# Two-layer decode kernel with backward pass: PSUM tiles of one bank for transposes, another order of zero stores and of streamed output-projection chunks, and vectors loaded as rows

## The chip, the core and the metric

The kernel runs on one NeuronCore of a Trainium2 chip. The metric is the device time of one execution in microseconds (us), as the median of several runs. One execution was also recorded by the hardware profiler; its trace gives the start and the length of every instruction and of the data transfers (DMA).

The engines named below are TensorE (PE, matrix multiplication; its weight loads are listed apart as PEld), VectorE (DVE), ScalarE (ACT), GpSimd (POOL) and SyncE (SP). Each has an instruction stream of its own and runs it in order. SP and ACT issue one kind of DMA queue, POOL another. PSUM, the memory that TensorE writes to, has 8 banks of 2 KiB per partition, and 128 partitions.

## The reference

One token (batch 1, sequence 1, width D = 1024) goes through attention, MLP, attention, MLP, each with a layer norm ahead and a residual sum behind, and both attentions use the same weights, as do both MLPs. The output and the gradients of everything but one unused input are returned.

```python
def _A_ref(x, k_cache, v_cache, wq, wo):          # Hq=32, Hkv=4, Sk=32768, Dh=128
    W = min(4096, max(256, Sk // 4))              # 4096: only the last W keys are used
    q = (x @ wq) ...                              # wq 1024 x 4096
    k = jnp.repeat(k_cache[:, :, Sk - W:, :], rep, axis=1); v = ...
    p = softmax(q k^T * Dh ** -0.5);  o = p v
    return o.reshape(B, Sq, Hq * Dh) @ wo         # wo 4096 x 1024
def _B_ref(x, w1, b1, w2):                        # F = 3584
    h = x @ w1 + b1;  act = h * tanh(softplus(h))
    return act @ w2
x = x + _A_ref(_layernorm(x), ...);  x = x + _B_ref(_layernorm(x), ...)
x = x + _A_ref(_layernorm(x), ...);  x = x + _B_ref(_layernorm(x), ...)
_out, _vjp = jax.vjp(_f, A_x, A_k_cache, A_v_cache, A_wq, A_wo, B_w1, B_b1, B_w2)
return (_out, *_vjp(grad_out))
```

All data are bf16. The gradients of the two caches have 4 x 32768 x 128 elements each, of which only the last 4096 positions of each head group are not zero; the other 28672 positions have to be written as zeros.

## The kernel before

The kernel has five parts, run one after the other by the data they need: the forward layers A1 (attention), B2 (MLP), A3 (attention), B4 (MLP); the backward layers B4, A3, B2, A1; and at the end the weight gradients, which are outer products of vectors kept from the layers (the "gradient part" below). Every vector of a layer is a column over 128 partitions.

**Weights.** wq, K and V are loaded once and stay in SBUF; so do the first 8 of 16 chunks of wo (`NR = 8`). The other 8 chunks of wo, and all of w1 (16 chunks of 448 KB) and w2 (14 chunks of 512 KB), are streamed anew in every layer through a pool `strm` of `NB = 5` buffers. SP issues these loads in the order of the program, each as soon as its buffer is free, so the first five chunks of a stage are requested before the stage begins.

**Forward.** `fwd_rows2` (L258) multiplies a chunk by a vector: 16 weight loads and 16 matmuls with one column each. In A1 and A3 the loop over the 16 wo chunks goes from 0 to 15, the kept ones first.

**Backward.** The backward products need the transposed chunks. `xpose2` (L153) transposes 16 blocks of 128x128 on TensorE into one PSUM tile of two banks, and then two copies (`evac`, L126), each of half the tile, bring them back into the same SBUF buffer; `evac` gives each copy to DVE or ACT by running sums of cost numbers. The backward stages (`mlp_bwd_w2`, `mlp_bwd_w1`, `attn_bwd`) run as a pipeline of lag 1: transposes of chunk i, then the products of chunk i-1. wq, K and V are transposed once for the backward pass: `attn_fwd` of A3 puts 32 such groups into a list `xq`, and `fill(n)` (L182) takes n from it. In the kernel before, 8 are taken between the wo chunks of A3 and 24 between the w1 chunks of B4 forward.

**PSUM.** Pool `p2` has 3 tiles of two banks, used for transposes, for the attention scores (`big`) and for small things; `pacc` holds two accumulators of one bank. For the gradient part `pacc` is released and a fourth two-bank tile takes its place.

**Zeros.** The 2 x 28672 x 4 zero rows are 112 stores of 512 KB from one SBUF tile `zt`. `zeros(n)` (L120) issues the next n of them on SP, so they stand in SP's queue among the loads. Where they stand is written out in the program: a table `Z` for the place after the fifth load of a stage, and single stores in the loops. The stores that are left go out at `zeros(1000)` behind the last backward layer.

**Gradient part.** Its pieces come in the order w2 (14 output tiles of 512 KB), b1, w1 (16 of 448 KB), wo (16), V cache (8), K cache (8), wq (16). Each tile is made by TensorE in PSUM, copied by DVE and ACT to one of 10 SBUF tiles, and stored by a DMA that POOL issues. `rows_put` (L585) prepares the vectors of a piece.

**Vectors.** x, grad_out and b1 are loaded straight into columns, by DMAs whose pieces are one or two elements long; the gradient of b1 is stored in the same way.

## Time and profile before

| | |
|---|---|
| median of 3 runs | 590.47 us (587.74 to 594.37) |
| profiled execution | 590.49 us; its span, first to last instruction, 588.5 us |
| busy: PE, DVE, ACT, POOL | 391.1, 227.7, 193.7, 51.6 us |
| DMA | 188.74 MB, mean 321 GB/s |
| mean granted TensorE clock | 0.67 of full speed |

Busy shares are averages over stages that are very unlike: long stages in which data streams in, chains of small dependent instructions, and the gradient part, which mostly writes. The DMA row of the profile's 40 slices (14.7 us each) and the rows of single stages say more. "[2.40 <-DMA w_c<-in_B_w_dram]" behind a row means that the engine was idle for 2.40 us ahead of it and that this load ended the wait; "issue" stands for idle time in which it waited for nothing that the profile shows.

The landmarks in the trace before, from DVE's rows: output of A1 at 74.83 us, of B2 at 115.60, of A3 at 164.29, of B4 at 232.09; end of the four backward layers at about 263, 317, 377 and 431 us; then the gradient part until 588.5.

### The profile page before, as it was taken

How to read it: one execution, taken by the hardware profiler on the slowest of the kernel's cores; microseconds unless marked ns; L12 is line 12 of the kernel's file. 1: busy time of each engine (PE TensorE's matmuls, PEld its weight loads, DVE VectorE, ACT ScalarE, POOL GpSimd, SP SyncE). 2: the span in 40 equal slices, each digit the busy share in tenths (PEclk: the TensorE clock that was granted, in tenths of full speed). 3: DMA queues.
4: the chain of work that ended last, by engine and by line, in shares of the span. 5: the costliest groups of instructions: out<-in, count | busy, mean ns of one | idle time of the engine just before them, and what ended most of it. 6: DMA issues, size and time to landing. Idle time of an engine off the chain costs nothing. (4 is left out here: it accounts for less than half of the span.)

```text
span 588.5 us, 15785 instructions
## 1 busy us (share of the span) xinstructions
PE 391.1 (66%) x7052; PEld 309.9 (53%) x7052; DVE 227.7 (39%) x409; ACT 193.7 (33%) x211; POOL 51.6 (9%) x95
## 2 busy tenths in 40 slices
PE   2375634476889789779679877886665313878871
PEld 2264533355879789668659866783611001136510
DVE  1033001012346633445422434333066415776692
ACT  1022000001436433435202333230055614755591
POOL 2000000000000000000000000000022212233341
PEclk9997555555869887979756889675555555555555
DMA  8999999993499698994921889999999999998886
GB/s 278 298 421 411 332 374 361 406 412 146 143 359 405 243 355 304 339 353 160 338 91 46 290 256 321 377 335 418 415 417 419 420 171 421 420 407 306 282 322 255
DMA packets 54883, 188.74 MB, mean 321 GB/s; under 512 B 9760, under 2 KB 9760, under 8 KB 53792
## 3 DMA queue, kind: packets, MB, share of 16 engines
q1 hardware_dynamic: 41648, 147.87, 67.4%
q0 software_dynamic: 10320, 39.86, 18.2%
q8 instruction: 55, 0.90, 0.6%
q10 hardware_dynamic: 2848, 0.01, 0.3%
q14 instruction: 12, 0.10, 0.1%
HBM read 89.14 MB, written 98.58 MB: 319 GB/s over the span
## 5 line engine op out<-in xcount | busy, mean ns | idle before, releaser
L177 PEld LDWEIGHTS <-w_c 128*128 128x128 bf16 x1792 | 59.2, 100 | 42.7 <-DMA w_c<-in_B_w_dram 23.8
L158 PE MATMUL tps<-ident_bf,w_c 128*128 128x128 bf16 x896 | 71.5, 244 | 12.7 <-DMA w_c<-in_B_w_dram 12.7
L132 ACT COPY w_c<-tps 128x1024 bf16<-128x1024 bf16 (+1 forms) x50 | 46.2, 927 | 82.7 <-DVE w_c L129 39.6
L129 DVE COPY w_c<-tps 128x1024 bf16<-128x1024 bf16 (+1 forms) x70 | 45.4, 667 | 67.7 <-PE tps L158 36.8
L158 PEld LDWEIGHTS <-w_c 128*128 128x128 bf16 x896 | 61.8, 111 | 14.0 <-DMA w_c<-in_B_w_dram 13.9
L132 ACT CAST st_t<-ops 128x1024 bf16<-128x1024 f32 x32 | 31.6, 1014 | 25.4 <-PE ops L177 19.7
L129 DVE CAST st_t<-ops 128x1024 bf16<-128x1024 f32 x28 | 33.6, 1223 | 9.7 <-issue 3.3
L177 PE MATMUL ops<-R_7920 2*128 2x512 bf16 (+1 forms) x64 | 11.1, 544 | 28.8 <-DVE st_w_8051 L129 6.4
L177 PE MATMUL acc<-a_pair,w_c 128*128 128x1 bf16 x448 | 15.7, 165 | 15.7 <-DMA w_c<-in_B_w_dram 10.3
L177 PE MATMUL acc<-nB_pair,w_c 128*128 128x1 bf16 x448 | 16.2, 165 | 14.4 <-DMA w_c<-in_B_w_dram 11.4
L158 PE MATMUL tps<-ident_bf,wo_c 128*128 128x128 bf16 x256 | 22.1, 256 | 3.6 <-DMA wo_c<-in_A_wo_dram 3.6
L177 PEld LDWEIGHTS <-wo_c 128*128 128x128 bf16 x512 | 16.7, 101 | 11.2 <-DMA wo_c<-in_A_wo_dram 6.9
L129 DVE COPY wo_c<-tps 128x1024 bf16<-128x1024 bf16 x20 | 13.5, 689 | 23.4 <-PE tps L158 16.0
L579 POOL DMA_DIRECT2D out_dram<-rt x2 | 1.2, 594 | 241.8 <-DVE rt L578 241.8
L129 DVE CAST st_kv<-ops 128x1024 bf16<-128x1024 f32 x15 | 18.3, 1224 | 9.9 <-PE ops L177 7.0
L177 PEld LDWEIGHTS <-R_7920 2*128 2x128 bf16 x64 | 2.3, 100 | 37.3 <-issue 37.3
L132 ACT CAST st_kv<-ops 128x1024 bf16<-128x1024 f32 x17 | 17.0, 1014 | 14.1 <-PE ops L177 14.1
L177 PE MATMUL acc<-dh_pair,w_c 128*128 128x1 bf16 x448 | 18.3, 165 | 4.8 <-ACT w_c L132 3.3
L158 PEld LDWEIGHTS <-wo_c 128*128 128x128 bf16 x256 | 19.1, 117 | 4.0 <-DMA wo_c<-in_A_wo_dram 4.0
L132 ACT COPY wo_c<-tps 128x1024 bf16<-128x1024 bf16 x12 | 12.1, 1012 | 25.6 <-DVE wo_c L129 17.1
L177 PE MATMUL ops<-Ro 2*128 2x512 bf16 x64 | 17.0, 603 | 5.0 <-ACT st_t L132 3.0
L634 POOL DMA_DIRECT2D out_dram<-st_t x30 | 16.0, 534 | 32.3 <-DVE st_t L129 14.1
(492 smaller groups left out, 711.4 us busy)
## 6 DMA issues: line engine op xcount, KB each, us to landing
out_dram<-zt SPq DMA_DIRECT2D x112, 512.0 KB, 10.0
w_c<-in_B_w_dram SPq DMA_DIRECT2D x64, 448.0 KB, 5.7
w_c<-in_B_w_dram SPq DMA_DIRECT2D x42, 512.0 KB, 6.1
wo_c<-in_A_wo_dram SPq DMA_DIRECT2D x32, 512.0 KB, 6.7
out_dram<-st_t POOLq DMA_DIRECT2D x30, 512.0 KB, 11.9
out_dram<-st_kv POOLq DMA_DIRECT2D x16, 512.0 KB, 5.7
out_dram<-st_wq POOLq DMA_DIRECT2D x16, 512.0 KB, 4.8
K_170<-in_A_k_cache_dram SPq DMA_DIRECT2D x1, 1024.0 KB, 13.3
```

The costliest lines, as they stand in the source:

```text
L129: nc.vector.tensor_copy(out_ap, in_ap)
L132: nc.scalar.copy(out_ap, in_ap)
L158: nc.tensor.transpose(ps[:, 8 * i + b, :], ap, ident_bf[:])
L177: nc.tensor.matmul(out_ap, lhsT=lhsT, rhs=rhs, start=start, stop=stop, skip_group_check=True, **kw)
L579: nc.gpsimd.dma_start(out_flat.rearrange("(n p) -> n p", p=P), rt[0:n, :])
L634: nc.gpsimd.dma_start(out_v[c], st[:])
```

## The change

1. **PSUM.** `p2` is gone until the gradient part. In its place stand `pt` with four tiles of one bank, and `pbig` with one tile of two banks for the scores. `xpose2` now takes one one-bank tile for each half (8 blocks), so that a half can be copied when its own 8 transposes are done. Ahead of the gradient part `pacc`, `pbig` and `pt` are released and `p2` is made with four tiles of two banks.
2. **Zeros.** The same 112 stores stand at other places: 6 in A1 (0 before), 18 in A3 (14), 15 among the w1 chunks of B4 forward (9), 2 in each backward w1 stage (4), 19 in the backward w2 stage of B2 (1), 4 in the attention backward of A1 (8); B2 (1), w2 of B4 (6) and the attention backward of A3 (8) keep theirs. What is left for the end is 31 stores (57 before).
3. **wo order.** The loop over wo in A1 and A3 takes chunks 8 to 15 (streamed) first and 0 to 7 (kept) then. No `fill` stands in that loop; B4 forward takes two groups for each of its 16 w1 chunks.
4. **Vectors.** x, grad_out and b1 are loaded as rows of 256 or 512 bytes at the start, transposed on TensorE and copied out of PSUM. The gradient of b1 is made ahead of the gradient part, transposed, and stored as 14 rows of 512 bytes.

SP's queue around the wo chunks of A1, from the last kept chunk on. `wo_c`, `w_c` are streamed chunks, `out_dram<-zt` is a zero store. Before:

```order
33 L244 DMA wo_200<-in_A_wo_dram 128x2048
34 L244 DMA wo_c<-in_A_wo_dram 128x2048 x8
35 L255 DMA w_c<-in_B_w_dram 128x1792 x5
36 L122 DMA out_dram<-zt 128x2048
37 L255 DMA w_c<-in_B_w_dram 128x1792 x11
```

And now:

```order
33 L255 DMA wo_210<-in_A_wo_dram 128x2048
34 L255 DMA wo_c<-in_A_wo_dram 128x2048 x5
35 L129 DMA out_dram<-zt 128x2048 x6
36 L255 DMA wo_c<-in_A_wo_dram 128x2048 x3
37 L266 DMA w_c<-in_B_w_dram 128x1792 x5
38 L129 DMA out_dram<-zt 128x2048
```

Six stores now stand between the fifth and the sixth streamed chunk. The same queue from A3's streamed wo chunks to the first w1 chunks of B4 forward. Before:

```order
39 L244 DMA wo_c<-in_A_wo_dram 128x2048 x5
40 L122 DMA out_dram<-zt 128x2048 x14
41 L244 DMA wo_c<-in_A_wo_dram 128x2048 x3
42 L255 DMA w_c<-in_B_w_dram 128x1792 x2
43 L122 DMA out_dram<-zt 128x2048
44 L255 DMA w_c<-in_B_w_dram 128x1792 x2
```

And now:

```order
41 L255 DMA wo_c<-in_A_wo_dram 128x2048 x5
42 L129 DMA out_dram<-zt 128x2048 x18
43 L255 DMA wo_c<-in_A_wo_dram 128x2048 x3
44 L266 DMA w_c<-in_B_w_dram 128x1792 x3
45 L129 DMA out_dram<-zt 128x2048
46 L266 DMA w_c<-in_B_w_dram 128x1792
47 L129 DMA out_dram<-zt 128x2048
```

Four more stores stand ahead of the sixth wo chunk, and from the third w1 chunk on each load has a store behind it. The queue at the end of A3's backward attention (`wo_c`) and in the backward w2 stage of B2 (`w_c`, 128x2048). Before:

```order
94 L244 DMA wo_c<-in_A_wo_dram 128x2048
95 L122 DMA out_dram<-zt 128x2048
96 L249 DMA w_c<-in_B_w_dram 128x2048 x5
97 L122 DMA out_dram<-zt 128x2048
98 L249 DMA w_c<-in_B_w_dram 128x2048 x9
```

And now:

```order
102 L255 DMA wo_c<-in_A_wo_dram 128x2048
103 L129 DMA out_dram<-zt 128x2048
104 L260 DMA w_c<-in_B_w_dram 128x2048 x5
105 L129 DMA out_dram<-zt 128x2048 x19
106 L260 DMA w_c<-in_B_w_dram 128x2048 x9
```

Nineteen stores instead of one stand between the fifth and the sixth w2 chunk. The core of the diff:

```diff
@@ -69,7 +69,8 @@
-    p2 = ctx.enter_context(tc.tile_pool(name="p2", bufs=3, space=bass.MemoryType.PSUM))
+    pt = tc.alloc_tile_pool(name="pt", bufs=4, space=bass.MemoryType.PSUM)
+    pbig = tc.alloc_tile_pool(name="pbig", bufs=1, space=bass.MemoryType.PSUM)
@@ -91,18 +92,24 @@
-    x0b = keep.tile([P, TD], BF16, name="x0b")
-    nc.sync.dma_start(x0b[:], A_x[0, 0, :].rearrange("(t p) -> p t", p=P))
+    rows0 = work.tile([P, 512], BF16, name="rows0", tag="e32", padded_shape=[P, 2 * WC])
+    x_row, g_row, b_row = rows0[0:TD, 0:P], rows0[0:TD, P:2 * P], rows0[0:NW2, 2 * P:4 * P]
+    nc.sync.dma_start(x_row, A_x[0, 0, :].rearrange("(t p) -> t p", p=P))
+    nc.scalar.dma_start(g_row, grad_out[0, 0, :].rearrange("(t p) -> t p", p=P))
+    nc.scalar.dma_start(b_row, B_b1.rearrange("(c x) -> c x", x=2 * P))
-    x0 = keep.tile([P, TD], FP32, name="x0")
-    nc.vector.tensor_copy(x0[:], x0b[:])
+    x0 = keep.tile([P, TD], FP32, name="x0")
+    xps = pt.tile([P, 1024], BF16, name="xps", tag="pt")
+    nc.tensor.transpose(xps[:, 0:TD], x_row, ident_bf[0:TD, 0:TD])
+    nc.vector.tensor_copy(x0[:], xps[:, 0:TD])
@@ -142,23 +149,27 @@
-    turn = [0]
+    def psum1(shape, dtype, name):
+        if "p2" in pools:
+            return psum2(shape, dtype, name)
+        return shaped(pt.tile([P, 512 if dtype == FP32 else 1024], dtype, name=name, tag="pt"), shape)
-        turn[0] += 1
-        pool = pools["p2b"] if "p2b" in pools and turn[0] % 4 == 0 else p2
-        t = pool.tile([P, 1024 if dtype == FP32 else 2048], dtype, name=name, tag="p2")
-        return shaped(t, shape)
+        if "p2" in pools:
+            return shaped(pools["p2"].tile([P, 1024 if dtype == FP32 else 2048], dtype, name=name, tag="p2"), shape)
+        return shaped(pbig.tile([P, 1024 if dtype == FP32 else 2048], dtype, name=name, tag="big"), shape)
-        ps = psum2([P, 16, P], BF16, "tps")
-        for i, (blocks, dst) in enumerate(halves):
+        pss = []
+        for blocks, dst in halves:
+            ps = psum1([P, 8, P], BF16, "tps")
-                nc.tensor.transpose(ps[:, 8 * i + b, :], ap, ident_bf[:])
-        for i, (blocks, dst) in enumerate(halves):
+                nc.tensor.transpose(ps[:, b, :], ap, ident_bf[:])
+            pss.append(ps)
+        for (blocks, dst), ps in zip(halves, pss):
-            evac(dst, ps[:, 8 * i:8 * i + n, :].rearrange("p b c -> p (b c)"), 0.08 * n + 0.03, 0.11 * n + 0.15)
+            evac(dst, ps[:, 0:n, :].rearrange("p b c -> p (b c)"), 0.08 * n + 0.03, 0.11 * n + 0.15)
...
@@ -390,24 +401,23 @@
         nc.vector.tensor_copy(o_nat[:], oacc[:])
-        ops = psum2([HQ, P], BF16, "ops")
+        ops = psum1([HQ, P], BF16, "ops")
         nc.vector.tensor_copy(o_row[:], ops[:, 0:P])
-        pps = psum2([P, 2, NO], FP32, "pps")
+        pps = psum1([P, 2, NO], FP32, "pps")
         yacc = acc_tile(TD)
-        for c in range(NO):
+        order = list(range(NR, NO)) + list(range(NR))
+        for i, c in enumerate(order):
             w = wo_kept[c] if c < NR else wo_load(c)
-            if c == NR + NB - 1:
+            if i == NB - 1:
                 zeros(Z["A1" if first else "A3"])
-            fwd_rows2(yacc, w, c, o_bf, c == 0, c == NO - 1)
-            if not first:
-                fill(1 if c % 2 else 0)
+            fwd_rows2(yacc, w, c, o_bf, i == 0, i == NO - 1)
@@ -427,8 +437,8 @@
             if g_bf is not None:
-                zeros(i % 2)
-                fill(2 if i % 2 else 1)
+                zeros(1 if i >= 2 else 0)
+                fill(2)
@@ -503,7 +513,7 @@
             ws[i] = w
-            zeros(1 if i % 4 == 3 else 0)
+            zeros(1 if i % 8 == 7 else 0)
@@ -524,7 +534,7 @@
                 loaded[c + NR] = wo_load(c + NR)
-                zeros(1)
+                zeros(1 if first or c % 2 else 0)
...
@@ -665,7 +675,7 @@
-    Z = dict(A1=0, B2=1, A3=14, B4=1, bw2=1)
+    Z = dict(A1=6, B2=1, A3=18, B4=1, bw2=19)
...
@@ -688,10 +697,14 @@
-        nc.scalar.dma_start(b1_b[:].rearrange("p (c t) -> p c t", t=2), B_b1.rearrange("(c p t) -> p c t", p=P, t=2))
-        nc.scalar.dma_start(gcolb, grad_out[0, 0, :].rearrange("(t p) -> p t", p=P))
-        nc.vector.tensor_copy(b1_f[:], b1_b[:])
-        nc.vector.tensor_copy(gcol[:], gcolb)
+        gps = psum1([P, TD], BF16, "gps")
+        nc.tensor.transpose(gps[:], g_row, ident_bf[0:TD, 0:TD])
+        nc.vector.tensor_copy(gcolb, gps[:])
+        nc.vector.tensor_copy(gcol[:], gps[:])
+        bps = psum1([P, 2, 16], BF16, "bps")
+        for t in range(2):
+            nc.tensor.transpose(bps[:, t, 0:NW2], b_row[:, t::2], ident_bf[0:NW2, 0:NW2])
+        nc.vector.tensor_copy(b1_f[:].rearrange("p (c t) -> p t c", t=2), bps[:, :, 0:NW2])
@@ -720,16 +733,21 @@
+    db1 = work.tile([P, 2, NW2], BF16, name="db1")
+    nc.vector.tensor_add(db1[:], sB4["dh"][:].rearrange("p (c t) -> p t c", t=2), sB2["dh"][:].rearrange("p (c t) -> p t c", t=2))
+    db_row = work.tile([NW2, P, 2], BF16, name="db_row", tag="e32", padded_shape=[NW2, WC, 2])
+    for t in range(2):
+        dbps = psum1([NW2, P], BF16, "dbps")
+        nc.tensor.transpose(dbps[:], db1[:, t, :], ident_bf[:])
+        nc.vector.tensor_copy(db_row[:, :, t], dbps[:])
+    nc.gpsimd.dma_start(out_7.rearrange("(c x) -> c x", x=2 * P), db_row[:].rearrange("c p t -> c (p t)"))
-    pools["p2b"] = ctx.enter_context(tc.tile_pool(name="p2b", bufs=1, space=bass.MemoryType.PSUM))
+    pbig.release()
+    pt.release()
+    pools["p2"] = ctx.enter_context(tc.tile_pool(name="p2", bufs=4, space=bass.MemoryType.PSUM))
-    db1 = work.tile([P, TF], FP32, name="db1")
-    nc.vector.tensor_add(db1[:], sB4["dh"][:], sB2["dh"][:])
-    db1_bf = work.tile([P, TF], BF16, name="db1_bf")
-    nc.vector.tensor_copy(db1_bf[:], db1[:])
-    nc.gpsimd.dma_start(out_7.rearrange("(c p t) -> p c t", p=P, t=2), db1_bf[:].rearrange("p (c t) -> p c t", t=2))

```

All other calls of `psum2` outside the gradient part and the scores become `psum1`.

More of the change, by code (lines that the diff above doesn't have):

```diff
@@ L284, in row_layout @@
         x = work.tile([P, G, DH], BF16, name=name, tag="rx", bufs=2)
-        ps = psum2([P, P], BF16, "rps")
+        ps = psum1([P, P], BF16, "rps")
         nc.tensor.transpose(ps[:, 0:P], col32[:], ident_bf[:])
@@ L319, in to_kpart @@
     def to_kpart(src, name):
-        ps = psum2([P, TJ, P], BF16, "kps")
+        ps = psum1([P, TJ, P], BF16, "kps")
         for j in range(TJ):
@@ L535, in attn_bwd @@
         nc.vector.tensor_copy(do_p[:], dacc[:].rearrange("p (c t) -> p t c", t=2))
-        dps = psum2([HQ, P], BF16, "dps")
+        dps = psum1([HQ, P], BF16, "dps")
         nc.tensor.transpose(dps[:, 0:P], do_p[:].rearrange("p t c -> p (t c)"), ident_bf[:])
@@ L541, in attn_bwd @@
         drf = dr[:].rearrange("h p t -> h (p t)")
-        qps = psum2([P, NO, 2], FP32, "qps")
+        qps = psum1([P, NO, 2], FP32, "qps")
         for e in range(2):
@@ L574, in col_out @@
     def col_out(cols, n, out_flat):
-        ps = psum2([2 * HQ, P], BF16, "rw")
+        ps = psum1([2 * HQ, P], BF16, "rw")
         nc.tensor.transpose(ps[0:n, 0:P], cols, ident_bf[:])
@@ L603, in rows_put @@
                     nc.vector.tensor_copy(spread[:, 4 * a:4 * a + 2, 3, l], v[:, 12:14])
-        ps = psum2([P, 8, P], BF16, "rw")
+        ps = psum1([P, 8, P], BF16, "rw")
         for j in range(8):
@@ L677 @@
     fold = work.tile([P, 32], FP32, name="fold")
-    b1_b = work.tile([P, TF], BF16, name="b1_b")
     b1_f = keep.tile([P, TF], FP32, name="b1_f")
```

## Prediction

> **What bounds the kernel now.** I read the page's DMA row first, then SP's own timeline, then stretches of the span chosen by it.
>
> ```profile
> span 588.5 us, 15785 instructions
> ...
> DMA  8999999993499698994921889999999999998886
> ```
>
> The DMA engines are full through the forward layers A1 and B2 (slices 1 to 9) and from slice 27 on, but nearly empty around slices 10, 21 and 22. SP's queue says why (start, length, count):
>
> ```profile
> 115.97 14.04 SPq L122 DMA_DIRECT2D out_dram<-zt  x14
> 153.68 2.02 SPq L244 DMA_DIRECT2D wo_c<-in_A_wo_dram  x3
> ...
> 293.13 0.56 SPq L122 DMA_DIRECT2D out_dram<-zt  x1
> 319.59 14.65 SPq L249 DMA_DIRECT2D w_c<-in_B_w_dram  x9
> ...
> 388.30 102.91 SPq L122 DMA_DIRECT2D out_dram<-zt  x58
> ```
>
> SP issues nothing from 293.7 to 319.6 us: the five buffers are full and A3's backward chain has to end first. And 58 zero stores go out at the end, for 103 us, in competition with the gradient part's output. Stretches of the span (length; busy time of PE, PEld, DVE, ACT, POOL; granted clock, DMA share, GB/s):
>
> ```profile
> 0.00:20.00 20.00, 5.30 (x130) 4.54 (x130) 2.74 (x18) 1.78 (x3) 3.04 (x10) 1.00 0.79 236
> 40.00:60.00 20.00, 13.25 (x245) 10.54 (x244) 7.92 (x13) 6.47 (x8) 0.23 (x1) 0.76 1.02 413
> ...
> 144.00:152.00 8.00, 7.41 (x173) 7.41 (x173) 2.17 (x5) 2.02 (x2) 0.00 (x0) 0.66 0.01 2
> ...
> 296.00:320.00 24.00, 19.46 (x474) 17.25 (x463) 5.15 (x13) 2.69 (x4) 0.23 (x1) 0.50 0.12 45
> 388.00:428.00 40.00, 26.52 (x586) 22.16 (x583) 9.38 (x20) 5.09 (x8) 0.95 (x1) 0.55 1.03 416
> 472.00:480.00 8.00, 1.43 (x10) 0.31 (x8) 2.38 (x2) 1.79 (x2) 1.08 (x2) 0.50 1.17 104
> ```
>
> At 416 GB/s a 512 KB zero store costs 1.26 us of the DMA engines. The sum is made against the profiled execution: span 588.5, reported time 590.49, so 2.0 around the span; the median of the runs, 590.47, is the same.
>
> **Term A, the gradient part.** 26 stores less in its way, and the b1 gradient no longer written in 4-byte pieces.
>
> ```profile
> 431.14 1.41 PE L177 MATMUL ops<-R_7412 2*128 2x512 bf16 x8
> ...
> 450.32 0.32 DVE L592 COPY spread<-nB_pair 128x32 bf16<-128x32 bf16 x2
> ...
> 455.79 1.29 ACT L132 CAST st_w_7951<-ops 128x1024 bf16<-128x1024 f32 x1 [0.75 <-PE ops L177]
> ...
> 459.23 1.32 ACT L132 CAST st_w_7981<-ops 128x1024 bf16<-128x1024 f32 x1
> ...
> 485.23 1.01 ACT L132 CAST st_w_8051<-ops 128x768 bf16<-128x768 f32 x1 [6.01 <-DMA out_dram<-st_w_7951]
> ...
> 503.77 0.54 POOL L634 DMA_DIRECT2D out_dram<-st_t  x1 [3.80 <-DVE st_t L129]
> ...
> 509.66 0.53 POOL L634 DMA_DIRECT2D out_dram<-st_t  x1 [0.60 <-DVE st_t L129]
> ...
> 522.07 1.01 ACT L132 CAST st_t<-ops 128x1024 bf16<-128x1024 f32 x1 [0.27 <-DVE st_t L129]
> ```
>
> Where tiles are free, w1 output goes at (459.23 - 455.79)/3 = 1.15 us a tile and wo output at (509.66 - 503.77)/5 = 1.18. Later copies wait up to 6.01 us for an output DMA to give a tile back; in the stretch 472 to 480 the DMA engines are fuller than full at 104 GB/s, which is the b1 gradient. Without such waits: w2 14 x 1.18 = 16.5, preparation 455.79 - 450.32 = 5.5, w1 16 x 1.15 = 18.4, preparation again 5.5, wo 16 x 1.18 = 18.9, last copy 1.0; together 65.8 where 523.1 - 431.1 = 92 stand. Gain 26. Are the zeros gone by then? Before, 40 us x 416 GB/s / 524288 B = 32 stores went out from 388 to 428 us alone; now 32 remain there in all, so they end about when the gradient part starts, with up to eight in flight; I take 1 us off: **-25**. The 23 MB of these three pieces need 55 us at 416 GB/s, less than 65.8. From 523 us on nothing changes, since the copies there wait for PE. Bounds: -30 to -15, the low end if zeros still hold half of the DMA engines for the first 20 us.
>
> **Term B, from the start to B2's end.**
>
> ```profile
> 20.78 0.59 PE L177 MATMUL acc<-nA_pair,wq_0_154 128*128 128x1 bf16 x16 [3.68 <-DMA wq_0_154<-in_A_wq_dram]
> ...
> 74.20 0.59 PE L177 MATMUL acc<-o_pair,wo_c 128*128 128x1 bf16 x16 [2.11 <-DMA wo_c<-in_A_wo_dram]
> ```
>
> The first 20 us move 236 GB/s where 413 is possible, a loss of 20 x (1 - 236/413) = 8.6 us, of which I leave 2.3 for the first latency: row loads give 6.3. The few small transposes that replace them lie ahead of the first weights' landing. But six stores, 7.5 us, now stand in SP's queue ahead of the last three wo chunks, and those come first in PE's order too; A1's last wait (2.11, on such a chunk) stays. The stage is bound by transfers up to 115.6 us, so the sum is -6.3 + 7.5, less some 1.7 in which the DMA was not full between 64 and 72: **-0.5**, between -5 and +4.
>
> **Term C, A3's output projection and B4's w1.**
>
> ```profile
> 144.87 0.57 PE L177 MATMUL acc<-o_pair,wo_186 128*128 128x1 bf16 x16 [0.29 <-DVE o_pair L402]
> 145.30 0.56 PE L177 MATMUL acc<-o_pair,wo_188 128*128 128x1 bf16 x16
> ...
> 157.45 0.55 PE L177 MATMUL acc<-o_pair,wo_c 128*128 128x1 bf16 x16 [0.41 <-DMA wo_c<-in_A_wo_dram]
> ...
> 161.77 1.87 PE L158 MATMUL tps<-ident_bf,wq_1_152 128*128 128x128 bf16 x16
> ...
> 166.88 0.51 PE L177 MATMUL acc<-nB_pair,w_c 128*128 128x1 bf16 x14 [1.50 <-DVE nB_pair L202]
> ...
> 175.35 1.06 PE L158 MATMUL tps<-ident_bf,wq_1_164 128*128 128x128 bf16 x16
> 176.25 0.49 PE L177 MATMUL acc<-nB_pair,w_c 128*128 128x1 bf16 x14
> 176.60 1.05 PE L158 MATMUL tps<-ident_bf,wq_0_166 128*128 128x128 bf16 x16
> ...
> 194.99 1.95 PE L158 MATMUL tps<-ident_bf,V_184 128*128 128x128 bf16 x32
> ```
>
> A wo chunk takes 0.43 us from start to start. Now the five loaded chunks run first, the sixth load is asked for at 145.3, lands 3.8 us later (153.68 to 157.45 before), two more follow at 1.26, and nine chunks at 0.43 end at about 155.5; with 3 us for sum and norm, w1 begins near 158.5 instead of 166.88: -8.4. The 18 stores end 5 us later than 14 did, still ahead of 145. In w1 a transposed group costs 0.90 (175.35 to 176.25) and a chunk 0.35. Before: 24 x 0.90 + 16 x 0.35 = 27.2 of 30.1 us, the rest mostly groups at the low clock (1.87). Now 32 x 0.90 + 16 x 0.35 + 2.9 = 37.3: +7.2. Loads and stores there are 15.2 MB, 36.5 us at 416 GB/s, but five chunks (5.5 us) come ahead, so PE is late last. **-1**, between -4 and +4 (stores delaying a chunk). [...]
>
> **Term D, backward stages.** PE's waits from 231.6 to 398.7 us (total, times, longest):
>
> ```profile
> PE tps L158 <- DMA w_c<-in_B_w_dram: 12.7, 14, 2.4
> PE acc L177 <- ACT w_c L132: 4.4, 13, 0.5
> PE tps L158 <- DMA wo_c<-in_A_wo_dram: 3.6, 4, 2.2
> PE acc L177 <- DVE w_c L129: 2.0, 7, 0.4
> PE acc L177 <- DVE wo_c L129: 1.7, 5, 0.4
> ```
>
> Copies are waited for 8.1 us. With a bank of its own the first half can be copied while the second is still being transposed, 0.45 us earlier; I take half, -4. Four banks hold two groups where six held three; at 0.45 us a half and copies on two engines that is enough while both engines run. Loads are waited for 16.3 us, and 8 of the stores that stood in front of them go; I take a quarter, -4. **-8**, between -14 and 0.
>
> **Term E, A3's backward chain beside 18 more stores.** They take 18 x 1.26 = 22.7 us and fit the 24 us stretch from 296 on, so the next loads wait little. But A1's same chain already runs beside stores:
>
> ```profile
> q8 instruction: 55, 0.90, 0.6%
> ...
> 422.19 0.21 PE L177 MATMUL acc<-dq_pair,wq_1_152 128*128 128x1 bf16 x2 [2.47 <-issue]
> ...
> 428.39 0.21 PE L177 MATMUL acc<-dq_pair,wq_1_168 128*128 128x1 bf16 x2 [2.63 <-issue]
> ```
>
> Twice PE stands still for nothing but "issue", 256 instructions apart, and instructions come by DMA too (queue q8). Copied to A3: **+5**, between 0 and +6. [...]
>
> **Term F, the handover.** Ahead of the first outer product now stand the b1 gradient's sum, two transposes and two copies, and all old PSUM tiles must be released; at 0.2 to 0.3 us each (0.32 in the row at 450.32) about **+1**, between 0 and +3.
>
> Sum: -25 - 0.5 - 1 - 8 + 5 + 1 = -28.5; the span becomes 560.0, the time **562**.
>
> **Rivals.** (1) Zeros in front of loads. If the idle stretches cannot take them, each of the 26 moved stores delays a load by 1.26 us: +32.8 - 25 + 5 = +12.8, or 603 us. It decides once more than 20 of 26 (25/1.26) lie on the path. For it: B's six do, and SP's queue is in order. Against: the rows of 144 to 152 and 296 to 320 (2 and 45 GB/s), which hold 4 and 18 of them. [...] Chance 0.05. (2) The gradient part gains only half, because its stores and the rest of the zeros still share the engines: +13 on the forecast, 575. Against: 414 to 416 GB/s were reached with both. 0.15. (3) Backward waits nearly vanish (-16 instead of -8) and the chain in A3 does not stall (-5): 549. 0.17. (4) The smaller PSUM groups do nothing or hold PE, as a copy on ACT takes 1.0 us and only two groups fit: D is 0, 570. 0.10. My forecast within 6 us either way: 0.53.
>
> **Range and chances.** The range ends at the centres of rivals 3 and 2 and so holds 0.53 + 0.10 + half of 0.32 = 0.79: 549 to 575. A change under 1% (5.9 us) is about what cannot be told from none. Faster by over 1%: 0.93; within: 0.03; slower: 0.04, rival 1 nearly alone.
>
> **What would show it.** Head: wq_0_154's counterpart waits under 1 us. Gradient part: 92 us to the last wo copy become about 67, no copy waits over 2 us for a DMA, and no stretch is full at 104 GB/s. B4's w1 takes 37 us and starts 8 earlier relative to A3's attention. A3's backward chain shows two waits on "issue" near 2.5 us. Waits on copies halve. The forecast is wrong if the zeros at the end reach far into the gradient part, if loads wait behind stores in A1 or the backward w2 stage, or if output stays slow without zeros.

## The result, and the profile after

The changed kernel takes 562.5 us (median of 4 runs, 562.3 to 563.8); the kernel before took 589.1 (4 runs, 583.1 to 594.4). The ratio is 0.959, with a 95% interval of 0.951 to 0.966. The profiled execution reported 562.27 us for a span of 560.3, so 2.0 us lie around the span, as before. Stage lengths, here and below, come from one profiled execution of each kernel, which can lie off the median of its runs: 12 us above it without stores in A1 (565.5 against 553.9), 2 to 7 above with six buffers, kept chunks first, zeros and pieces, and tiles of two banks, and 5 below with the zeros put back.

The page's DMA row, in 40 slices of the span:

```profile
span 560.3 us, 15939 instructions
...
DMA  8999989999799979789599888896998978797986
```

The two holes of before, around slices 10 and 21, are filled, and the row is no longer full without a break from slice 27 on. The same stretches of the span as in the prediction (length; busy time of PE, PEld, DVE, ACT, POOL; granted clock, DMA share, GB/s):

```profile
0.00:20.00 20.00, 6.97 (x166) 5.95 (x166) 3.48 (x19) 1.78 (x3) 3.04 (x10) 1.00 0.90 337
40.00:60.00 20.00, 8.82 (x198) 7.12 (x190) 4.00 (x9) 1.79 (x3) 0.23 (x1) 0.63 1.02 409
144.00:152.00 8.00, 4.28 (x134) 3.84 (x130) 0.60 (x3) 0.00 (x0) 0.00 (x0) 0.50 0.53 173
296.00:320.00 24.00, 15.14 (x424) 13.43 (x415) 4.46 (x12) 1.10 (x3) 0.23 (x1) 0.57 1.01 409
388.00:428.00 40.00, 24.08 (x530) 19.91 (x530) 9.07 (x26) 3.61 (x6) 0.95 (x1) 0.61 1.02 408
472.00:480.00 8.00, 4.93 (x27) 1.76 (x29) 4.65 (x7) 4.70 (x5) 1.07 (x2) 0.50 0.44 175
```

The head moves 337 GB/s instead of 236, A3's backward chain (296 to 320) 409 instead of 45, and the stretch around 476 us that was overfull at 104 GB/s is idle half of the time. SP's queue shows where the zero stores went (start, length, count):

```profile
54.13 6.68 SPq L129 DMA_DIRECT2D out_dram<-zt  x6
...
117.71 21.18 SPq L129 DMA_DIRECT2D out_dram<-zt  x18
...
292.24 23.26 SPq L129 DMA_DIRECT2D out_dram<-zt  x19
322.40 13.86 SPq L260 DMA_DIRECT2D w_c<-in_B_w_dram  x9
...
385.76 38.46 SPq L129 DMA_DIRECT2D out_dram<-zt  x32
```

The last 32 have all been issued at 424.2 us, before the first outer product, and only 0.9 MB of them, less than two stores, still moves after it. So the gradient part runs nearly without them. These are its rows on PE, ACT, DVE and POOL: its first matmuls, the first w1 copy and the fourth, DVE's last six wo copies in one row, and the wo outputs one and six.

```profile
428.79 1.05 PE L188 MATMUL ops<-R_7572 2*128 2x512 bf16 x8 [0.54 <-DVE db_row L742]
```

```profile
451.68 1.29 ACT L139 CAST st_w_8092<-ops 128x1024 bf16<-128x1024 f32 x1 [0.75 <-PE ops L188]
...
455.12 1.33 ACT L139 CAST st_w_8122<-ops 128x1024 bf16<-128x1024 f32 x1
```

```profile
488.09 7.11 DVE L136 CAST st_t<-ops 128x1024 bf16<-128x1024 f32 x6 [0.19 <-ACT st_t L139]
```

```profile
477.91 0.54 POOL L644 DMA_DIRECT2D out_dram<-st_t  x1 [6.34 <-DVE st_t L136]
...
483.79 0.53 POOL L644 DMA_DIRECT2D out_dram<-st_t  x1 [0.60 <-issue]
```

A w1 tile takes (455.12 - 451.68)/3 = 1.15 us, a wo tile (483.79 - 477.91)/5 = 1.18: the pace that the prediction took from the undisturbed stretches of before. No copy waits for a DMA any more. From the first outer product to the end of the last wo copy on either engine it is 488.09 + 7.11 - 428.79 = 66.4 us, where the kernel before has 92.2. All lengths of the gradient part below are measured so; the expectations on record take earlier ends, most of them the start of ACT's last copy row (63.8 and 90.9 us).

What got worse is in A1. PE's rows there are the last chunk of wq, then the first and the sixth streamed chunk of wo:

```profile
26.52 0.58 PE L188 MATMUL acc<-nA_pair,wq_1_178 128*128 128x1 bf16 x16 [0.69 <-DMA wq_1_178<-in_A_wq_dram]
...
57.97 0.59 PE L188 MATMUL acc<-o_pair,wo_c 128*128 128x1 bf16 x16 [4.09 <-DMA wo_c<-in_A_wo_dram]
...
71.67 0.59 PE L188 MATMUL acc<-o_pair,wo_c 128*128 128x1 bf16 x16 [8.08 <-DMA wo_c<-in_A_wo_dram]
```

The head wins 4 us (30.5 before), but the sixth chunk waits 8.08 us behind the six stores. In the backward part, PE's waits between 232.6 and 394.9 us (total, times, longest) have changed sides:

```profile
PE tps L168 <- DMA w_c<-in_B_w_dram: 16.0, 16, 2.1
PE tps L168 <- DMA wo_c<-in_A_wo_dram: 5.6, 4, 2.0
PE acc L188 <- issue: 4.3, 2, 2.6
...
PE acc L188 <- ACT w_c L139: 0.7, 2, 0.4
```

Waits on ACT's copies of w_c fell from 4.4 to 0.7 us; waits on loads rose from 16.3 to 21.6 although eight stores fewer stand in front of them. The "issue" line is new, and belongs to A3's chain (the first two rows; the other two are A1's chain, as before):

```profile
309.53 0.24 PE L188 MATMUL acc<-dq_pair,wq_1_154 128*128 128x1 bf16 x3 [1.70 <-issue]
315.73 0.24 PE L188 MATMUL acc<-dq_pair,wq_1_170 128*128 128x1 bf16 x3 [2.62 <-issue]
...
418.10 0.30 PE L188 MATMUL acc<-dq_pair,wq_1_162 128*128 128x1 bf16 x6 [2.72 <-issue]
424.57 0.30 PE L188 MATMUL acc<-dq_pair,wq_1_178 128*128 128x1 bf16 x6 [2.92 <-issue]
```

Stage by stage, from marks that both traces have (x after B2, the product a in B4, the last sums of each stage, the first outer product, the last copy of wo), in us:

| stage | before | after | difference | predicted |
|---|---|---|---|---|
| start to x after B2 (B) | 115.6 | 117.3 | +1.7 | -0.5 |
| A3 and B4's w1 (C) | 84.3 | 82.1 | -2.2 | -1 |
| six backward stages (D) | 177.0 | 169.6 | -7.4 | -8 |
| A3's backward chain (E) | 21.8 | 25.8 | +4.0 | +5 |
| A1's backward chain | 30.0 | 30.1 | +0.1 | 0 |
| handover (F) | 2.5 | 3.9 | +1.4 | +1 |
| gradient part (A) | 92.2 | 66.4 | -25.8 | -25 |
| from there to the end | 65.2 | 65.1 | -0.1 | 0 |

The spans differ by 28.2 us (the rows add up to 28.3), forecast -28.5. The sum being right says nothing yet about the causes inside each row.

### The profile page after: what moved, and what is told of

It is laid out like the page before. It is cut to its first block, busy times and chain, and to the rows that moved or that the text cites. A ratio compares the mean times of both kernels' runs of the same rounds, so it can differ in the third digit from the quotient of the medians.

```text
span 560.3 us, 15939 instructions
## 1 busy us (share of the span) xinstructions
PE 384.5 (69%) x7058; PEld 305.6 (55%) x7058; DVE 228.9 (41%) x411; ACT 192.4 (34%) x211; POOL 51.0 (9%) x95
## 3 DMA queue, kind: packets, MB, share of 16 engines
q1 hardware_dynamic: 40624, 147.87, 69.9%
## 5 line engine op out<-in xcount | busy, mean ns | idle before, releaser
L168 PE MATMUL tps<-ident_bf,w_c 128*128 128x128 bf16 x896 | 72.9, 246 | 16.3 <-DMA w_c<-in_B_w_dram 16.0
L139 ACT CAST st_t<-ops 128x1024 bf16<-128x1024 f32 x32 | 31.3, 1014 | 23.4 <-PE ops L188 21.6
L188 PEld LDWEIGHTS <-wo_c 128*128 128x128 bf16 x512 | 16.4, 102 | 22.6 <-DMA wo_c<-in_A_wo_dram 21.8
L188 PE MATMUL acc<-a_pair,w_c 128*128 128x1 bf16 x448 | 15.8, 165 | 17.2 <-DMA w_c<-in_B_w_dram 12.3
L209 ACT ACTIVATE lnv<-var,eps_t 128x1 f32<-128x1 f32 x4 | 1.2, 294 | 72.5 <-DVE var L206 72.5
L188 PE MATMUL acc<-o_pair,wo_c 128*128 128x1 bf16 x256 | 8.7, 166 | 21.2 <-DMA wo_c<-in_A_wo_dram 20.9
L136 DVE COPY wo_c<-tps 128x1024 bf16<-128x1024 bf16 x20 | 13.7, 691 | 21.2 <-PE tps L168 20.6
L136 DVE CAST st_wq<-ops 128x1024 bf16<-128x1024 f32 x15 | 17.2, 1217 | 1.8 <-ACT st_wq L139 0.8
```

Source lines behind the costliest of these rows:

```text
L136: nc.vector.tensor_copy(out_ap, in_ap)
L139: nc.scalar.copy(out_ap, in_ap)
L168: nc.tensor.transpose(ps[:, b, :], ap, ident_bf[:])
L188: nc.tensor.matmul(out_ap, lhsT=lhsT, rhs=rhs, start=start, stop=stop, skip_group_check=True, **kw)
L209: nc.scalar.activation(lnv[:], var[:], ACT.Ln, bias=eps_t[:, 0:1], scale=1.0)
```

## Experiments

Twelve kernels were run. All are edits of the changed kernel, so "undone" means one part put back as it was before. Times are medians of 4 or 5 runs; the ratio is to the kernel before on the same chip. The kernel before itself came to medians from 585.0 to 589.1 us beside them, so a difference of less than about 4 us between two of these kernels isn't shown by the times alone. Nor do the traces part small differences: where the code is the same, x after B2 comes at 117.3 to 118.8 us (the changed kernel, the one with b1 pieces, the one with one store beside A3's chain, the one with the loop stores back), and the six backward stages take 166.7 to 171.0 us (the changed kernel, b1 pieces, columns, kept chunks first) and 176.3 (no stores in A1).

### Zero stores back

```
-    Z = dict(A1=6, B2=1, A3=18, B4=1, bw2=19)
+    Z = dict(A1=0, B2=1, A3=14, B4=1, bw2=1)
-                zeros(1 if i >= 2 else 0)
+                zeros(i % 2)
-            zeros(1 if i % 8 == 7 else 0)
+            zeros(1 if i % 4 == 3 else 0)
-                zeros(1 if first or c % 2 else 0)
+                zeros(1)
```

> The changed kernel with every zero store back where it was before (A1 0, A3 14, backward w2 1, and one per two, four and one loads in the loops); vectors, PSUM and wo order stay changed. Theory, the sum of the prediction: the zeros make most of term A. The gradient part, 65.8 us long in the changed kernel from the first outer product to the last wo copy, grows by 20 to 26 us; A1 and B2 get 6 to 7.5 us shorter, A3's backward chain 4 us shorter (25.84 back to about 21.8, no waits on issue over 1 us there). 562.5 + 23 - 7 - 4 = about 575 us. Rival: the b1 gradient in 4-byte pieces, not the zeros, held the output DMA; then the gradient part stays below 72 us and the time comes to 562.5 + 5 - 11 = about 557.

Measured 569.2 us, ratio 0.977 (0.970 to 0.983). The copies wait for tiles again; a row of DVE's in the gradient part, and DVE's last wo copies:

```profile
458.31 1.29 DVE L136 CAST st_w<-ops 128x1024 bf16<-128x1024 f32 x1 [4.95 <-DMA out_dram<-st_t]
...
490.50 7.11 DVE L136 CAST st_t<-ops 128x1024 bf16<-128x1024 f32 x6 [0.20 <-ACT st_t L139]
```

From the first outer product (414.03) to the end of the last wo copy (497.61) it is 83.6 us against 66.4: 17 us, a little under the theory's 20. x after B2 comes 7.1 us earlier and A3's chain takes 21.3 us, as expected. The surprise is the balance: moving the stores gains 17 us at the end and hands back 7.1 in A1 and 4.5 in A3's chain. In this trace the six backward stages are 4.2 us shorter, too, which is no more than the scatter. The time stayed 6 us below the theory's 575. By the medians the placement of the zeros is worth 7 us of the 27.

### The b1 gradient in 4-byte pieces, alone and with the zeros

```
-    nc.gpsimd.dma_start(out_7.rearrange("(c x) -> c x", x=2 * P), db_row...)
...
+    nc.gpsimd.dma_start(out_7.rearrange("(c p t) -> p c t", p=P, t=2), db1_bf...)
```

> The changed kernel with the b1 gradient written as before, in 4-byte pieces behind the w2 gradient. Theory: the pieces keep the DMA engines busy for some 8 us at a quarter of their rate (104 GB/s at 1.17 before), a loss of about 6 us of transfers; ten stage tiles hide some of it, so +2 to +6 us: 564 to 568, less 0.5 to 1 us for the handover that becomes shorter (3.88 back towards 2.5). Rival: the pieces were the main reason for the waits of 6 us on output tiles; then the gradient part grows by 12 us or more, 575. Second rival: hidden entirely, 561 to 562.

Measured 562.6 us, ratio 0.966 (0.957 to 0.974): hidden entirely. The gradient part is 66.6 us against 66.4, and the handover 1 us shorter.

> The changed kernel with both the zero stores and the b1 gradient's 4-byte pieces as before; head, PSUM and wo order stay changed. Alone, the pieces cost 0.2 us of the gradient part (64.0 against 63.8 us from the first outer product to the last wo copy) and the zeros 17 (81.0). Theory, an interaction: the pieces cost only where the DMA engines are full; then the part takes 88 to 92 us, as in the kernel before (90.9), and the time is 577 to 581. Rival, the costs add: 81 to 82 us and 569 to 571; then the other 10 us of the kernel before came from elsewhere, for instance from when its zeros began.

Measured 574.0 us, ratio 0.978 (0.972 to 0.985); the part took 91.6 us (419.06 to 510.70), as in the kernel before (92.2). A copy of ACT's in it:

```profile
469.83 1.01 ACT L139 CAST st_w<-ops 128x768 bf16<-128x768 f32 x1 [5.28 <-DMA out_dram<-st_t]
```

So it is an interaction: 0.2 us by the pieces alone, 17.2 by the zeros alone, 25.2 by both, which is nearly all of term A. The pieces cost 8 us beside the zeros and 0.2 without them: the DMA share of the part is 0.85 in the changed kernel (428.79 to 495.20 us), and 1.03 in the kernel before (431 to 523), which has both. The time is 3 us below the theory's range.

### PSUM tiles of two banks again

```
-    pt = tc.alloc_tile_pool(name="pt", bufs=4, ...)     # one bank each
-    pbig = tc.alloc_tile_pool(name="pbig", bufs=1, ...)
+    pt = tc.alloc_tile_pool(name="pt", bufs=3, ...)     # two banks each, for all
```

> The changed kernel with three PSUM tiles of two banks for all transposes, as before; zeros, vectors and wo order stay changed. Theory (term D as predicted): the waits of PE on copies between 232 and 395 us come back from about 1 us to 8, and half or more of it is paid: +4 to +7 us in the backward stages, 567 to 570 us; K's transposes in A1 end up to 7 us later, without effect on x_A1 since loads bind there. Rival: the copies' waits come back but the loads' waits (16.0 and 5.6 us) fall by as much, since PE simply reaches the next load later; the time stays at 562 to 564.

Measured 568.9 us, ratio 0.973 (0.962 to 0.983). The six backward stages take 176.7 us, as long as in the kernel before (177.0), and not 169.6. PE's waits from 233.1 to 403.7 us:

```profile
PE tps L168 <- DMA w_c<-in_B_w_dram: 10.0, 10, 2.8
PE tps L168 <- DMA wo_c<-in_A_wo_dram: 4.6, 4, 1.6
...
PE acc L188 <- DVE w_c L135: 3.4, 11, 0.5
PE acc L188 <- ACT w_c L138: 2.7, 9, 0.5
```

Both halves of the two theories hold: the waits on copies are back, and the waits on loads are a third lower (14.6 against 21.6), since PE comes later to the next chunk. But the time follows the first theory. The finer tiles are worth some 6 us by the medians and 7 in these traces, which is about all of term D. The intervals of the two ratios touch, and 7 us of length is near the scatter named above, so this size is less sure than the return of the waits. In the traces it is more than the waits by themselves give: in the six backward stages and A3's chain, PE's busy time differs by 6.8 us (162.9 against 156.1) at nearly the same mean clock (0.77 in both). What shortens PE's own work there is not settled.

### Loads of vectors as columns again

```
-    nc.sync.dma_start(x_row, A_x[0, 0, :].rearrange("(t p) -> t p", p=P))
+    nc.sync.dma_start(x0b[:], A_x[0, 0, :].rearrange("(t p) -> p t", p=P))
     (grad_out and b1 in the same way, without the transposes)
```

> The changed kernel with x, grad_out and b1 loaded as columns, as before (2-byte and 4-byte pieces). Theory: the first 20 us fall from 337 to about 236 GB/s, the last chunk of wq is used 4 us later (26.5 back to 30.5), and since the loads bind up to the end of B2, the 4 to 6 us are paid in full: x_B2's addition at 121 to 123 instead of 117.3, time 566 to 568.5. Rival: there is slack between the loads and PE in A1 and B2, x_B2 stays within 1.5 us of 117.3 and the time at 562 to 564.

Measured 567.0 us, ratio 0.974 (0.967 to 0.982). The first 20 us:

```profile
0.00:20.00 20.00, 5.30 (x130) 4.53 (x130) 2.74 (x18) 1.78 (x3) 3.04 (x10) 1.00 0.78 237
```

237 GB/s, and x after B2 at 124.5 instead of 117.3 us, later than the theory's 121 to 123: the 7 us of the head are paid in full as far as B2's end. 4.5 us of them are left in the median, as the theory had it.

### Kept wo chunks first again

```
-        order = list(range(NR, NO)) + list(range(NR))
+        order = list(range(NO))
...
+            if not first:
+                fill(1 if c % 2 else 0)
```

> The changed kernel with the kept wo chunks first, as before, in A1 and A3, and the 8 groups of wq, K and V transposes that filled A3's wo chunks back there; zeros, vectors and PSUM stay changed. Theory (term C as measured, -2.2 us from B2's end to the product a in B4): A3's wo part gets longer by about 8 us and B4's w1 shorter by 6 to 7, so +1 to +3 there; in A1 the wait of 8.08 us for the sixth streamed chunk is hidden behind the kept ones, but it only moves: x_B2 within 1 us of 117.3. 563.5 to 566 us. Rival: in A1 the kept chunks cover the six zero stores and 2 to 4 us are gained there, the time is 559 to 562.

Measured 566.4 us, ratio 0.960 (0.951 to 0.970), so the medians lean to the theory and the interval can't part it from no difference. In the trace the order works both ways: x after B2 comes 1.8 us earlier with the old order, and A3 with B4's w1 takes 89.9 us instead of 82.1. With the zeros of before (the first experiment) the new order's stage took 81.8, and the kernel before took 84.3. So the new order saves at most about 2.5 us in itself, and up to 8 once ten more stores must fit into that stage: with the old order PE then waits 5.6 us for loads in B4's w1, with the new one for none.

### No zero stores in A1

```
-    Z = dict(A1=6, B2=1, A3=18, B4=1, bw2=19)
+    Z = dict(A1=0, B2=1, A3=18, B4=1, bw2=19)
```

> The changed kernel with no zero stores in A1; the six go to the end of the program's zeros (38 instead of 32 there). Theory: loads bind up to B2's end, so the six stores are paid there in full: the wait of 8.08 us for the sixth chunk falls to about 1, x_B2's addition comes 6 to 7.5 us earlier (110 to 111.5); at the end the 38 stores end 7.5 us later, about 432, and the first outputs share the DMA engines with them, which ten stage tiles take with 0 to 3 us: 556 to 559 us. Rival, the mechanism of term A: each store left at the end costs about what it did before (26 us for 26 stores), so +6 at the end and the time stays at 561 to 564.

Measured 553.9 us, ratio 0.941 (0.935 to 0.948): faster than the changed kernel. PE's rows for the first and the sixth streamed chunk of A1:

```profile
58.09 0.58 PE L188 MATMUL acc<-o_pair,wo_c 128*128 128x1 bf16 x16 [4.23 <-DMA wo_c<-in_A_wo_dram]
...
64.38 0.59 PE L188 MATMUL acc<-o_pair,wo_c 128*128 128x1 bf16 x16 [0.66 <-DMA wo_c<-in_A_wo_dram]
```

The wait of 8.08 us is gone: x after A1 comes 7.3 us earlier (71.0 against 78.3). x after B2 is 5.1 us earlier in this trace (112.3), less than the theory had. The 38 stores at the end cost 1.2 us of the gradient part (67.6 against 66.4). The median is 2 us below the theory's range, and its gain of 8.6 us more than the stores' 7.5; where the rest comes from isn't shown. So the first places at the end are nearly free, and the stores in A1, where loads already fill the DMA engines (a share of 1.01 from 54 to 72 us in this run, which stores no zeros there), were a plain loss.

### One store beside A3's backward chain

```
-    Z = dict(A1=6, B2=1, A3=18, B4=1, bw2=19)
+    Z = dict(A1=6, B2=1, A3=18, B4=1, bw2=1)
```

> The changed kernel with one zero store instead of 19 beside A3's backward chain; the 18 go to the end (50 instead of 32). Theory: the chain has no wait on issue over 1 us and takes 21.8 instead of 25.84 us (-4); the end pays 18 stores at 0.7 to 1.0 us, +13 to +18: 571 to 577. [...]

Measured 568.9 us, ratio 0.969 (0.962 to 0.977), below the range of the theory, since the end pays less than it had. A3's chain takes 21.8 us, as the theory had it, and its 256 matmuls against wq run as one piece:

```profile
304.49 6.97 PE L188 MATMUL acc<-dq_pair,wq 128*128 128x1 bf16 x256 [0.28 <-ACT dq_pair L573]
```

The two waits on "issue" belong to the stores beside the chain, as term E had it. At the end the gradient part grows by 10.7 us for 18 stores. Together with the other runs that gives its length by the number of stores left for the end: 24 or 32 stores 66.4 us, 38 67.6, 50 77.1, 58 83.6. From 38 on a store costs 0.8 us, and by that slope below some 36 nothing: with 32 left the part goes at the pace of its tiles, 1.15 and 1.18 us each, at a DMA share of 0.85, so the last few stores find room there. What counts is what is still unwritten at the first outer product: 0.9 MB of zeros with 32 stores, 3.8 with 38, 9.5 with 50, 13.7 with 58.

### No zero stores at all

```
-            nc.sync.dma_start(zero_jobs.pop(0), zt[:])
+            zero_jobs.pop(0)
```

> The changed kernel without any zero store: the zero rows of the gradients of the K and V caches are not written, everything else is. It tells what all the zero stores still cost. Theory: 7 us in A1 and B2, 4 in A3's backward chain, 3 to 5 in A1's (two stalls on issue), 4 to 8 of the waits on loads in the backward stages (16.0 and 5.6 us), none in the gradient part: 562.5 - 20 = 540 to 545 us. Rival: the waits on loads in the backward stages are not due to the stores but to five buffers and the latency of a load; then they stay within 3 us of 21.6 in sum and the time is 546 to 551.

Measured 523.5 us, ratio 0.889 (0.881 to 0.897): what is left of the zeros' price is 39 us, twice the theory's 20. A1's chain (362.5 to 386.2) and its matmuls against wq:

```profile
362.50:386.20 23.70, 18.10 (x445) 14.71 (x445) 5.37 (x15) 2.00 (x4) 0.96 (x1) 0.52 0.01 2
```

```profile
379.11 7.01 PE L188 MATMUL acc<-dq_pair,wq 128*128 128x1 bf16 x256
```

No matmul of the program waits on "issue" any more. The 39 us are 7.6 up to B2's end, 1.8 in A3 and B4's w1, 18.7 in the six backward stages, and 10.8 in the two chains. Of the 21.6 us of waits on loads 15.2 stay: 6.4 less, as the theory's 4 to 8 had it, so the rival with 3 less at most is out (with B4's w2, 15.9 stay of 24.9). But the stages shrink by more than the waits do: the clock granted there is higher as well (mean over the six 0.90 instead of 0.80; over the whole execution 0.698 instead of 0.671).

### Eight stores back in the backward loops

```
-            zeros(1 if i % 8 == 7 else 0)
+            zeros(1 if i % 4 == 3 else 0)
-                zeros(1 if first or c % 2 else 0)
+                zeros(1)
```

> The changed kernel with only the loops' zero stores back (one per four chunks in both backward w1 stages, one per wo load in A1's backward): 8 stores more in front of loads, 24 instead of 32 at the end. Theory, term D's second half: the loads behind them are later, the backward w1 stages and A1's output part together 3 to 5 us longer; A1's chain up to 1 us shorter: 565 to 567. Rival: PE waits for a load there for its latency, not for those stores; the three stages stay within 1.5 us of 81.4 in sum (30.35, 28.79, 22.24), the time at 560 to 563.

Measured 559.0 us, ratio 0.954 (0.946 to 0.962). The three stages take 81.2 us in sum, against 81.4: the rival. Eight stores less in front of the loads gave nothing. Term D's second half, -4, was wrong. The time is 1 us below the rival's range and 3.5 below the changed kernel, of which A1's chain gives 1.8 (28.3 against 30.1); a gain this small is not shown by the times.

### Smaller zero stores, and a sixth buffer

Two last kernels, both without stores in A1. The first halves each zero store, and moves two small tiles of the gradient part to other memory; the second has a sixth stream buffer besides.

```
-    ZC = 2048
+    ZC = 1024
-        for _ in range(min(n, len(zero_jobs))):
+        for _ in range(min(2 * n, len(zero_jobs))):
-        x = work.tile([P, G, DH], BF16, name=name, tag="rx", bufs=2)
+        x = pools["rows"].tile([P, G, DH], BF16, name=name, tag="rx", bufs=2)
   (second kernel only)
-NB = 5
+NB = 6
```

> The changed kernel without zero stores in A1 (553.9 us by itself) and with six stream buffers instead of five; room comes from the zero tile, now half as wide (each zero store in two of 256 KB), and from two tiles of the last part that move to space freed by V. Theory: in the backward stages PE waits for loads that start one buffer too late; of 24.9 us of waits from B4's w2 to A1's output part in the changed kernel, 8 to 12 go, the clock rises with them, and the time is 541 to 547. Rival: the loads share the DMA engines with the zero stores, and a sixth buffer only queues them earlier; waits stay above 20 us, the time at 551 to 556.

> The changed kernel without zero stores in A1 and with each zero store in two of 256 KB from a zero tile half as wide, as in the run with six buffers, but with five buffers. That run came to 523.6 us, 30 below the one with five buffers and stores of 512 KB (553.9). Theory, the size of the stores: smaller stores let loads and instruction blocks through sooner; waits on issue in A3's and A1's chains stay near 1.3 and 0.7 us, waits on loads from B4's w2 to A1's output part fall by a third or more from 24.9, and the time is 522 to 532. Rival, the sixth buffer: loads then wait as in the changed kernel (22 us or more), only the chains gain (3 and 5 us), and the time is 544 to 552. In between, 533 to 543: both carry a part, read from the two sums of waits.

Measured: half stores 546.9 us, ratio 0.935 (0.927 to 0.943); with six buffers 523.6, ratio 0.891 (0.885 to 0.896). So by the medians 553.9 becomes 546.9 by the size of the stores, and 523.6 by the buffer. The 30 us of the two together beat both theories of the kernel with six buffers; the other kernel, in its rival's range, shows that the buffer carries 23 of them and the size the other 7. The 23 are clear of noise. The 7 are not by the times alone, since the intervals of 0.941 (0.935 to 0.948) and 0.935 overlap.

The size acts on the chains: A3's takes 23.6 us and A1's 24.3 (26.1 and 29.4 in the kernel with whole stores and none in A1), with 1.5 and 0.4 us of waits on "issue" in them instead of 4.2 and 5.9. Against that, the gradient part takes 70.7 us instead of 67.6: A1's chain is shorter, and 7.3 MB of zeros are unwritten at the first outer product instead of 3.8. The buffer acts on the backward stages: 151.4 us instead of 166.6, with waits on loads of 12.8 instead of 20.2. The waits explain 7 of these 15 us. Another part goes with the granted clock. PE in the backward w1 stage of B4 with five buffers (the 14 transposes of a group; groups between left out):

```profile
228.90 0.96 PE L168 MATMUL tps<-ident_bf,w_c 128*128 128x128 bf16 x14 [1.13 <-DMA w_c<-in_B_w_dram]
...
230.44 1.68 PE L168 MATMUL tps<-ident_bf,w_c 128*128 128x128 bf16 x14 [0.26 <-DMA w_c<-in_B_w_dram]
...
232.89 1.67 PE L168 MATMUL tps<-ident_bf,w_c 128*128 128x128 bf16 x14 [0.42 <-DMA w_c<-in_B_w_dram]
...
236.84 1.66 PE L168 MATMUL tps<-ident_bf,w_c 128*128 128x128 bf16 x14
```

and the stretch 220 to 243 us, with five buffers and then with six:

```profile
220.00:243.00 23.00, 21.12 (x374) 20.69 (x372) 10.20 (x18) 9.91 (x12) 0.00 (x0) 0.70 0.86 269
```

```profile
220.00:243.00 23.00, 18.75 (x426) 18.23 (x423) 11.44 (x22) 11.14 (x13) 0.00 (x0) 0.97 0.95 336
```

With a few short waits among them, five groups on end, from 230.44 to 240.36 us, cost 1.67 us each instead of 0.96; the granted clock of the whole stretch is 0.70 with five buffers and 0.97 with six. The kernel with six buffers and half stores writes all outputs, zeros included, and is as fast as the changed kernel without any zeros.

## Why the prediction was right, and where it was not

The time was forecast at 562.0 and came at 562.5; faster by 4.1%, where faster by over 1% had 0.93. The mechanisms of the large terms held. That the sum came out within half a microsecond is luck: its terms missed by 0.4 to 2.2 us, in both directions, and the 95% interval of the result is some 9 us wide.

**Term A** (-25): measured -25.8, with the pace per tile, the end of the zeros and the absence of waits as written. What the prediction left open, the share of its two causes, is now known: 17 us the zeros alone, 0.2 the pieces alone, and 8 more only where both come together.

**Term B** (-0.5): mis-sized by 2 us. Its two large entries were right (row loads 6.3, measured 7.2; six stores 7.5, measured 7.1 in the first experiment). What failed are the credit "less some 1.7 in which the DMA was not full", which isn't seen, and the order of the wo chunks, which the sum had at nothing in A1 and which cost 1.8: with these, 117.3 = 115.6 - 7.2 + 7.1 + 1.8. Both are of the size by which this landmark scatters (117.3 to 118.8), so how the 2 us divide is not shown.

**Term C** (-1): measured -2.2, within its bounds. A3 got 7.6 us shorter (forecast 8.4 for the start of w1) and the stretch from x after A3 to the product a in B4 5.4 longer (35.6 to 41.0; forecast 7.2). That PE is late last in w1 held: between 158.45 and 199.41 us it waits for no load, and without any zero store the stretch is as long (40.8). Two groups ran at the low clock at its start (1.87 and 1.78 us; granted clock 0.50 from 160 to 164 us, 0.95 from 164 to 170), where three had (1.87, 1.87 and 1.91; 0.50 from 166 to 170, 0.72 from 170 to 176).

**Term D** (-8): right in sum (-7.4) by two errors that cancel. "I take half, -4" for the copies should have been -6 to -7 (the two-bank kernel); "I take a quarter, -4" for the loads should have been about 0 (the loop stores put back). That the two came to the right sum is luck. The mechanism of the second was wrong: waits on loads did not fall with the stores in front of them, they rose from 16.3 to 21.6 us. The two-bank kernel, with the new places of the stores, has 14.6: where PE waits for copies it comes later to each chunk. A gain on one wait turned partly into another.

**Term E** (+5): right, +4.0, and shown from both sides: 25.8 us with 19 stores beside the chain, 21.3 to 21.8 with one or none. The waits in the chains stand where the DMA share is 1.01 (296 to 320 us) and 1.03 (394.9 to 424.9), and not in the chain that had it at 0.01 (A1's, without zero stores). What these waits end on can be read from the DMA packets in the traces. Queue q8, of the kind "instruction" on the profile's page, moves 55 blocks of 16384 bytes. Between the two waits of each chain PE goes through 256 matmuls and weight loads, and its 14116 of the whole program make 55.1 times 256. In the changed kernel such a block ends at 308.09, 314.42, 416.60 and 423.32 us, and PE goes on 1.25 to 1.50 us later, at the four rows shown above. In the traces of the changed kernel and of the one before each of PE's eight waits on "issue" of over 1 us ends 1.25 to 1.50 us behind such a block. The four blocks took 0.92 to 0.96 us, no more than the mean of 1.04 over the 55 of this trace, so they were late rather than slow; what held them back before they started, the traces don't show.

**Term F** (+1): +1.4.

**The rivals.** Rival 1, zeros in front of loads, was right about A1 alone: six stores, 7.1 us, paid in full; of the other 20, the 18 beside A3's chain cost 4 us there, in waits on "issue" that end behind instruction blocks (1.70 and 2.62 us) and not in waits on loads, and the rest nothing that can be told from scatter. Rival 2 (gradient part gains half) is out; it would have needed more than 50 stores at the end, where 32 are. Rival 3 had one true half: the waits on copies nearly vanished; but the time did not follow, and the chain did stall. Rival 4 fell with the two-bank kernel.

## What to carry to other kernels

Here background stores were free only while something else set the pace: the gradient part took 66.4 us with 24 or with 32 of them left for the end, while six in A1, at a DMA share of 1.02 (40 to 60 us), cost 7.1 us. So put them where the DMA row is low, keep them out of a stage in which loads bind, and count how many the end can take before it starts to pay (here some 36 of 112, with a chain of 30 us to write them in). Where transposes wait for copies, first take the wait away, then look which wait stands behind it: here it was loads, and one more stream buffer was worth 23 us, most of what the whole change gave. When several terms of a sum are taken at "half" and "a quarter", each needs a kernel of its own in which it alone is undone, since errors in them can cancel without a trace in the total.

## What the hardware showed that was not expected

The size of the zero stores matters beside their bytes. With the same bytes in pieces of 256 KB instead of 512, waits on "issue" fell from 4.2 and 5.9 to 1.5 and 0.4 us in the two chains, and the median by 7 us. The packets of the stores' queue became smaller: queue q1 has 56752 of them in the kernel with half stores and six buffers, 40624 in the one with whole stores and none in A1, for the same 148 MB. How smaller stores shorten these waits, no run here shows.

The granted clock was 0.70 in a stretch whose waits are short (220 to 243 us, half stores and five buffers). A wait of 1.13 us and two shorter ones (0.26 and 0.42) go with five groups at 1.67 us instead of 0.96, so that stage lost more than the waits' own length. That the waits brought the clock down is not shown. In the kernel with six buffers (0.97 in the same stretch) groups behind waits of similar length in the same stage still took 0.96 us (PE's rows):

```profile
230.91 0.96 PE L168 MATMUL tps<-ident_bf,w_c 128*128 128x128 bf16 x14 [1.10 <-DMA w_c<-in_B_w_dram]
...
233.01 0.96 PE L168 MATMUL tps<-ident_bf,w_c 128*128 128x128 bf16 x14 [0.82 <-DMA w_c<-in_B_w_dram]
```

What decides between the two is not settled by these runs.
